# The second half of a w_in product in seven block products, with partial sums kept in PSUM, on one Trainium2 core

## The chip, the core and the metric

One core of a Trainium2 chip runs the whole program; tensors come from and go to HBM. The metric is the device time in microseconds (us) of one execution, of which several were run; the median is compared. 0.2% of it, about 1.5 us, is what counts here as a difference.

## What is computed

A layer norm, attention with a memory over four segments, and a gated MLP that mixes along the sequence. Cut to what matters here (x is 2048 x 1024; `_ln` is a layer norm over the last axis):

```python
h = x + A_ref(_ln(x))                     # 32 heads, 4 segments of 512 tokens, then @ wo
z = gelu(_ln(h) @ w_in)                   # 2048 x 3584
z1, z2 = z[:, :1792], _ln(z[:, 1792:])
g = w_sp @ z2 + b_sp[:, None]             # w_sp is 2048 x 2048
out = h + (z1 * g) @ w_out
```

The part that is changed is the second half of z, `z[:, 1792:]` before its layer norm: a product of 2048 x 1024 by 1024 x 1792, called z2 in the code. The first half is z1.

## The kernel before, in words

The code records every operation of five engines in Python, in the order in which it is called, finds what each has to wait for (by 32-byte cells of SBUF and by whole banks of PSUM, line 87), and then issues each engine's list in that order. So each engine, and each DMA queue, works strictly in the order of the calls. All operations have the line of the recorder, 210, in the profile; they are told apart by the names of their tiles. PE is TensorE, DVE VectorE, ACT ScalarE, POOL GpSimd, SP the engine whose queue issues most DMAs.

The stages, in order:

- **Attention**, n = 0 to 31: segment n // 8 and a group of four heads n % 8. Each round has three sets of logits on PE into banks 0 to 3, three Exp on ACT out of them (`e`), masks on POOL, P times V on PE (`pv`), the division on DVE (`norm`, line 631) into `otok`. Into the gaps of PE go "fills" f1 to f4: projections for the next round, tiles of the wo product of the segment before (`wo`, line 673, which adds x on DVE into `hch`, writes h to `out`, and queues a layer norm) and, in rounds 30 and 31, six groups of z2. `bg_pop` (line 690) moves each queued layer norm one step on: statistics on DVE, then the reciprocal root on POOL (`ln_rstd`, line 491), then the application on DVE (`lno`), followed by a transposing DMA into `HNT`, the normalised h with features on partitions.
- **The end of attention.** After round 31 come `pv(31)` on PE and `norm(31)` on DVE, then four transposing DMAs `oT<-otok`, which the wo product of the last segment reads.
- **z2** (lines 815 and 1019): 64 groups `(k, tc)`, 4 column blocks of 448 by 16 token blocks of 128, each of 8 matmuls of 448 columns, GELU on ACT, statistics on DVE (`z2_stats`). Between the first of them stand the wo tiles of the last segment. Beside it, in `aux`, run the norms of the two weights w_in (first half, on DVE, `sqz`) and w_sp (on ACT, `sj`), the scaling of w_in's first half to 16-bit floats (`wzh`), and differences of blocks of `HNT` (`hn_sum`, line 972).
- **z1** (line 1199): the first half, already by seven block products. With blocks of 512 features and 512 tokens, four output blocks come from seven products of 4 matmuls instead of eight. The factors need sums of blocks: `hn_sum` for h, `sz_sum` (line 985, on POOL) for w_in. DVE adds the products together (`zt<-ps,zt`), reading PSUM. The layer norm of z2 is applied here (`z2_apply`, line 839). w_sp is loaded, scaled and summed.
- **The gate** in two halves (w_sp times z2 by seven products, times z1) and **w_out** in two halves, the second by seven products.

`next_bank` (line 421) hands out the PSUM banks in turn. No operation of POOL touches PSUM here. In z1, bank by bank: product 1 is copied to SBUF by ACT and added to products 6, 7 and 4 by DVE.

Of the kernel before, what the change touches and what calls it, by code (L numbers as in the profile page):

```python
# [14 lines left out]
H = 32  # L15
# [243 lines left out]
def bass_sequential_preLN__memory_aug_infini_attn__mixer_gmlp__prompt_kernel(  # L259
# [31 lines left out]
    class Bump:  # L291
# [4 lines left out]
        def __call__(self, name, shape, dt):  # L296
# [50 lines left out]
    ZSTG = [tens("zstg%d" % i, [128, 448], F32, (134 + 2 * i) * K) for i in range(4)]  # L347
    XCH = [b2("xch%d" % i, [128, D], BF16) for i in range(4)]
# [4 lines left out]
    E = [[b2("e%d%d" % (k, i), [128, 4, w], BF16) for i, w in enumerate((512, 512, 256))] for k in range(2)]  # L353
    TA = b2("ta", [128, 4, 4, 32], F32)
    TM = [b2("tm%d" % i, [128, 4, 4, 32], F32) for i in range(2)]
    V = b2("v", [128, 4, H, 34], BF16)
    OTOK = [b2("otok%d" % i, [128, 4, D], BF16) for i in range(2)]


    WIN = [tens("win%d" % i, [128, 8, 512], BF16, o * K) for i, o in enumerate((46, 54, 190, 198))]  # L360
# [9 lines left out]
          for k, o in ROLES + (("t1", 118), ("t2", 190), ("t3", 22), ("t4", 38))}  # L370
    SS = tens("ss", [128, 4, 8, 128], F16, 30 * K)
    Z1X = tens("z1x", [128, 14, T], F16, 62 * K)
    HT = [{1: Z1X[:, 1:5, 1024:1536], 2: Z1X[:, 1:5, 1536:2048], 3: Z1X[:, 8:12, 1024:1536],
           4: Z1X[:, 8:12, 1536:2048]},
          {1: tens("ht1", [128, 4, L], F16, 190 * K), 2: tens("ht2", [128, 4, L], F16, 194 * K),
           3: tens("ht3", [128, 4, L], F16, 38 * K), 4: tens("ht4", [128, 4, L], F16, 198 * K)}]
    SZ = [tens("sz%d" % i, [128, 4, 128], F16, o * K) for i, o in enumerate((58, 59, 60, 61, 204))]
    ZT = [tens("zt%d" % i, [128, L], F32, o * K) for i, o in enumerate((4, 6, 8, 10, 202, 12))]
# [7 lines left out]
    SQ = b3("sq", [128, 16], F32)  # L386
    SQZ = b3("sqz", [128, 14], F32)
# [18 lines left out]
    SY = [tens("sy%d" % i, [128, 4, 7, 128], F16, o * K) for i, o in enumerate((190, 126))]  # L406
    FIN = [tens("fin%d" % i, [128, 512], BF16, o * K) for i, o in enumerate((37, 11, 12, 13))]
# [399 lines left out]
    CH = [(FH + 448 * k, 448) for k in range(4)]  # L807

    def win_load(k):
        lo, w = CH[k]  # L810
        sp.dma_start(WIN[k][:, :, 0:w], wcols(B_w_in, lo, lo + w))

    zs, zq, staged = [], [], []

    def z2_group(k, tc, stage=None):
        s, tcl = divmod(tc, 4)
        b = next_bank()
        wi = WIN[k]
        mm8(PS[:, b, 0:448], lambda i: HNT[s][:, i, tcl * 128:(tcl + 1) * 128], lambda i: wi[:, i, 0:448])
# [6 lines left out]
    def z2_gelu(k, tc, src):  # L826
        act.activation(Z2[:, tc, k * 448:(k + 1) * 448], src, ACTF.Gelu_apprx_tanh)
        zs.append((k, tc))

    def z2_stats():  # L830
        k, tc = zs.pop(0)
        dve.bn_stats(ZST[:, tc, k, :], Z2[:, tc, k * 448:(k + 1) * 448])
        if k == 3:
# [13 lines left out]

    LAST = NSEG * NQ - 1
    for n in range(LAST + 1):
# [15 lines left out]
        elif c < 6:  # L865
            f3, f4 = [("wo", s - 1, c - 2, 0)], [("wo", s - 1, c - 2, 1)]
        elif c == 6:
            f3, f4 = [("z2", 0, 4, 0)], [("z2", 0, 5, 1)]
        else:
            f1, f2 = [("z2", 0, 6, 2)], [("z2", 0, 7, 3)]  # L870
            f3, f4 = [("z2", 0, 0)], [("z2", 0, 1)]
# [14 lines left out]
        if n == 0:  # L886
# [3 lines left out]
            f3 = [("vmm", 0, 0, 1, 6, 2, 8), ("vout", 0, 0, 1, 6)]  # L890
        logits(n, 0)
# [24 lines left out]
        bg_pop()  # L916
        if n == 0:
# [616 lines left out]
```

## Time and profile before

| | us |
|---|---|
| median of 3 runs (754.47 to 755.01) | 754.56 |
| profiled execution, own time | 753.9 |
| its span, first to last instruction | 752.2 |
| busy in the span: PE / DVE / ACT / POOL | 747.5 / 559.3 / 421.3 / 297.0 |
| attention, up to the end of `pv(31)` | 0 to 302.8 |
| z2 and the last wo tiles | 302.8 to 404.3 |
| z1 | 404.3 to 490 |

The profile is a page and a trace of one execution. A timeline's line gives the start in us, the duration, the engine, the operation, the output and inputs by tile name, their shapes and the count of instructions merged into the line; in square brackets is the idle time of the engine before it, and who ended it. A matmul's duration is longer than the distance to the next matmul, since they are pipelined. The chain of waits follows the end of the program back to its beginning, at each step to whatever was waited for.

### The profile page before, as it was taken

The page shows a single profiled execution, that of the slowest core. Times are in us where ns is not written, and L with a number is a line of the kernel's source. Part 1 is how long each engine was busy: PE and PEld are TensorE (multiplying, and loading weights), DVE is VectorE, ACT ScalarE, POOL GpSimd, SP SyncE. Part 2 cuts the span into 40 slices and gives each one's busy share as a digit, 9 for nine tenths or more (in the row PEclk, how much of TensorE's full clock was granted, in tenths as well). Part 3 has the DMA queues.
Part 4 walks back from the last instruction along what each step waited for, and adds up shares of the span by engine and source line. Part 5 has one row for each costly group of instructions (what it writes and reads, how often), then busy time and mean ns, then how long its engine had stood idle before and what let it go on. Part 6 is the DMA issues. An engine that isn't in the chain of part 4 may idle for free.

```text
span 752.2 us, 13510 instructions
## 1 busy us (share of the span) xinstructions
PE 747.5 (99%) x5470; PEld 358.8 (48%) x5470; DVE 559.3 (74%) x1013; ACT 421.3 (56%) x519; POOL 297.0 (39%) x450
## 2 busy tenths in 40 slices
PE   8999999999999999999999999999999999999998
PEld 4445455555555445545554444444444444444444
DVE  5585589768975576667988796997885465989776
ACT  6777877787777767324994879733231445300000
POOL 2564456555654334010049888622220001222342
PEclk9999999999999999999999999999999999999999
DMA  9654556444523331669650027320019950001211
GB/s 303 177 159 88 85 82 135 99 74 91 120 58 81 118 84 44 162 178 262 196 169 0 1 45 138 56 98 1 0 23 155 269 185 28 0 1 43 78 50 57
DMA packets 136783, 75.09 MB, mean 100 GB/s; under 512 B 98064, under 2 KB 126480, under 8 KB 136720
## 3 DMA queue, kind: packets, MB, share of 16 engines
q1 hardware_dynamic: 129184, 67.14, 36.9%
q10 hardware_dynamic: 7536, 7.08, 3.3%
q8 instruction: 43, 0.70, 0.4%
q14 instruction: 20, 0.16, 0.1%
HBM read 42.74 MB, written 8.39 MB: 68 GB/s over the span
## 4 chain that ended last, share of the span: by engine, by line
PE 98%; DMA 1%; ACT 0%; DVE 0%; ACTq 0%; DVEq 0%; issue 0%
PE ps L210 98%; DMA wv<-in_A_wv_dram 1%; ACT L210 0%; DVE fin L210 0%; ACTq L210 0%; DVEq L220 0%; ACT rdm L210 0%
## 5 line engine op out<-in xcount | busy, mean ns | idle before, releaser
L210 ACT ACTIVATE e<-ps 128x2048 bf16<-128x2048 f32 (+1 forms) x96 | 152.6, 1590 | 41.7 <-PE ps L210 41.5
L210 POOL TENSOR_SCALAR_AFFINE_SELECT e<-e 128x512 bf16<-128x512 bf16 x128 | 90.6, 720 | 131.6 <-ACT e L210 131.5
L210 PE MATMUL ps<-win,hnT 128*128 128x448 bf16 x512 | 98.4, 352 | 0.0
L210 POOL TENSOR_TENSOR tmp_s1b<-tmp_s,brow 128x512 f32<-128x512 f32 x28 | 36.9, 1322 | 121.3 <-DVE tmp_u L210 62.5
L210 PEld LDWEIGHTS ps<-win,hnT 128*128 128x128 bf16 x512 | 49.6, 98 | 46.3 <-issue 0.2
L210 PE MATMUL ps<-xnT,wk 128*128 128x512 bf16 x256 | 60.8, 380 | 0.0
L210 PE MATMUL ps<-xnT,wq 128*128 128x512 bf16 x256 | 60.5, 379 | 0.0
L210 PE MATMUL ps<-wv,xnT 128*128 128x512 bf16 x256 | 59.7, 380 | 0.3 <-DVE xnT L210 0.3
L210 DVE TENSOR_TENSOR zt<-ps,zt 128x512 f32<-128x512 f32 x70 | 48.2, 690 | 15.6 <-PE ps L210 12.3
L210 PE MATMUL ps<-wo,oT 128*128 128x512 bf16 x256 | 58.0, 379 | 0.0
L210 ACT ACTIVATE z<-ps 128x448 bf16<-128x448 f32 x60 | 30.4, 545 | 33.4 <-PE ps L210 33.4
L210 PE MATMUL ps<-w_out,z1T 128*128 128x512 bf16 x224 | 48.6, 379 | 0.0
L210 PEld LDWEIGHTS ps<-v,e 128*128 128x128 bf16 x1280 | 38.8, 96 | 14.0 <-issue 6.5
L210 DVE BATCH_NORM_STATS2 zst<-z 128x6 f32<-128x448 bf16 x64 | 37.7, 607 | 7.8 <-ACT z L210 7.8
L210 DVE RECIPROCAL rd<-ps 128x16 f32<-128x16 f32 x32 | 8.0, 250 | 47.1 <-PE ps L210 46.9
L210 PE MATMUL ps<-v,e 128*128 128x33 bf16 x1280 | 42.2, 178 | 0.0
L210 ACT ACTIVATE tmp_s<-ps,invy 128x512 f32<-128x512 f32 x7 | 4.8, 688 | 64.9 <-POOL tmp_s1b L210 36.1
L210 POOL TENSOR_TENSOR sz<-wzh 128x512 f16<-128x512 f16 x28 | 34.4, 1230 | 16.9 <-DVE wzh L210 8.5
L210 PEld LDWEIGHTS ps<-wo,oT 128*128 128x128 bf16 x256 | 24.0, 98 | 27.6
L210 PEld LDWEIGHTS ps<-xnT,wk 128*128 128x128 bf16 x256 | 22.6, 98 | 29.9 <-issue 5.0
L210 ACT ACTIVATE z1T<-zt,inv 128x512 bf16<-128x512 f32 x42 | 29.0, 716 | 13.1 <-DVE zt L210 13.1
L210 PEld LDWEIGHTS ps<-wv,xnT 128*128 128x128 bf16 x256 | 23.1, 98 | 27.2 <-DVE xnT L210 0.7
(204 smaller groups left out, 1462.3 us busy)
## 6 DMA issues: line engine op xcount, KB each, us to landing
sj<-in_B_w_sp_dram SPq DMA_DIRECT2D x16, 512.0 KB, 3.5
xch<-in_A_x_dram SPq DMA_DIRECT2D x16, 256.0 KB, 3.5
xr<-in_A_x_dram SPq DMA_DIRECT2D x16, 256.0 KB, 4.0
out_dram<-hch SPq DMA_DIRECT2D x16, 256.0 KB, 2.5
win<-in_B_w_in_dram SPq DMA_DIRECT2D x4, 896.0 KB, 5.4
wz<-in_B_w_in_dram SPq DMA_DIRECT2D x6, 512.0 KB, 8.3
wo<-in_A_wo_dram SPq DMA_DIRECT2D x1, 2048.0 KB, 8.5
fin<-out_dram ACTq DMA_DIRECT2D x16, 128.0 KB, 3.0
```

The source lines that it names most:

```text
L210: ins = getattr(e, op.name)(*op.args, **op.kw)
```

## The change

z2 is made by the same seven-product scheme as z1, on blocks of 512 features, 512 tokens (in tiles of 128) and 448 columns. Eight of the 64 plain groups stay (six of them in attention), the other 56 output blocks come from 14 groups of seven products. `z2_step(q, k)` issues product k of group q; a list sorted by 7 q + OFF2[k] interleaves neighbouring groups, and `at(n, ...)` hangs other work behind its n-th step. Of the sums between products, some are made by PE itself: ACT copies product 1 from its bank into a second bank, and product 6 is accumulated onto it, then 7 or 4; ACT keeps copies after 6 and 5, and DVE adds them in after 7 and 3. Where a bank had not been written over the full width, one dummy matmul is issued into it first. Banks are handed out from a list `free`, and given back after products 2, 3 and 4.

For this w_in's second half, too, is scaled to 16-bit floats (`w_half`), and its blocks are summed (`w_sum`, `w_perm`). The scale must be known in attention, so w_in and seven sixteenths of w_sp are loaded there in pieces once more, or earlier, and their norms (a maximum on DVE, or squares on ACT) are taken there; the rest of w_sp follows in z2 by half rows. `hn_sum` for the first half of the tokens moves into attention, that for the second into z2. In z1 the feature blocks are taken in another order (`FC`), two of w_in's four scalings and some 17 statistics of z2 are done there. Many buffers lie at other addresses. Unchanged functions that only moved in the file are left out here.

```diff
...
-    ZSTG = [tens("zstg%d" % i, [128, 448], F32, (134 + 2 * i) * K) for i in range(4)]
-    XCH = [b2("xch%d" % i, [128, D], BF16) for i in range(4)]
+    ZSTG = [tens("zstg%d" % i, [128, 448], F32, int(o * K)) for i, o in enumerate((201, 202.75, 204.5, 144))]
...
-    HT = [{1: Z1X[:, 1:5, 1024:1536], 2: Z1X[:, 1:5, 1536:2048], 3: Z1X[:, 8:12, 1024:1536],
-           4: Z1X[:, 8:12, 1536:2048]},
-          {1: tens("ht1", [128, 4, L], F16, 190 * K), 2: tens("ht2", [128, 4, L], F16, 194 * K),
-           3: tens("ht3", [128, 4, L], F16, 38 * K), 4: tens("ht4", [128, 4, L], F16, 198 * K)}]
+    HT = [{1: Z1X[:, 0:4, 1024:1536], 2: Z1X[:, 0:4, 1536:2048], 3: Z1X[:, 4:8, 1024:1536],
+           4: Z1X[:, 4:8, 1536:2048]},
+          {1: tens("ht1", [128, 4, L], F16, 4 * K), 2: tens("ht2", [128, 4, L], F16, 8 * K),
+           3: tens("ht3", [128, 4, L], F16, 38 * K), 4: tens("ht4", [128, 4, L], F16, 200 * K)}]
+    WIN = {0: tens("win0", [128, 8, 448], BF16, 46 * K), 2: tens("win2", [128, 8, 448], BF16, 54 * K),
+           1: Z1T[:, 0:8, 0:448], 3: Z1T[:, 0:8, 448:896]}
+    WIH = {0: tens("wih0", [128, 8, 448], F16, 46 * K), 2: tens("wih2", [128, 8, 448], F16, 54 * K),
+           1: Z1X[:, 0:8, 0:448], 3: Z1X[:, 0:8, 448:896]}
+
+    WSO = {"a": 190, "b": 193.5, "c": 197, "d": 126, "e": 178, "f": 174.5, "g": 101, "h": 94, "i": 97.5}
+    WSO = {k: tens("ws" + k, [128, 4, 448], F16, int(o * K)) for k, o in WSO.items()}
+    WS = {pc: {k: WSO[x] for k, x in zip((2, 3, 4), ks)} for pc, ks in
+          (((0, 0), "abc"), ((1, 0), "abd"), ((0, 1), "efg"), ((1, 1), "hig"))}
+    ZP = [[tens("zp%d%d" % (p, i), [128, 448], F32, (o + 2 * i) * K) for i in range(6)]
+          for p, o in enumerate((162, 105))]
...
+    NB = [tens("nb%d" % i, [128, T], BF16, int(o * K)) for i, o in
+          enumerate((22, 26, 181.5, 185.5, 197.5, 201.5, 189.5, 193.5, 14))]
...
+    free = []
+
+    def next_bank(hold=False):
+        if free:
+            b = free.pop(0)
+            if not hold:
+                free.append(b)
+            return b
...
-        wi = WIN[k]
-        mm8(PS[:, b, 0:448], lambda i: HNT[s][:, i, tcl * 128:(tcl + 1) * 128], lambda i: wi[:, i, 0:448])
+        mm8(PS[:, b, 0:448], lambda i: HNT[s][:, i, tcl * 128:(tcl + 1) * 128], lambda i: WIH[k][:, i, :])
...
-        act.activation(Z2[:, tc, k * 448:(k + 1) * 448], src, ACTF.Gelu_apprx_tanh)
+        act.activation(Z2[:, tc, k * 448:(k + 1) * 448], src, ACTF.Gelu_apprx_tanh, scale=INV[1][:])
-        if k == 3:
+        nz[tc] = nz.get(tc, 0) + 1
+        if nz[tc] == 4:
...
+    def scale_in(src, n, w):
+        m = src[:, 0:n]
+        dve.scalar_tensor_tensor(m, m, float(w), m, ALU.mult, ALU.mult)
+        pool.tensor_copy(SQB[:, 0:src.shape[1]], src[:])
...
+    FC = (2, 3, 0, 1, 4, 5, 6, 0, 1, 2, 3, 4, 5, 6)
...
+    def w_half(c, eng=dve):
+        if eng is act:
+            act.activation(WIH[c][:], WIN[c][:], ACTF.Copy, scale=SC[1][:])
+            return
+        eng.tensor_single_scalar(WIH[c][:], WIN[c][:], SC[1][:], ALU.mult)
+
+    def w_blk(i, j, c):
+        return WIH[c + 2 * i][:, 4 * j:4 * j + 4, :]
+
+    def w_sum(c, k, ws=None, eng=dve):
+        if k == 1:
+            eng.tensor_tensor(w_blk(1, 0, c), w_blk(1, 0, c), w_blk(1, 1, c), ALU.add)
+            return
+        a, b = {3: (w_blk(0, 0, c), w_blk(1, 0, c)), 2: (w_blk(1, 1, c), ws[3][:]), 4: (w_blk(0, 1, c), ws[2][:])}[k]
+        eng.tensor_tensor(ws[k][:], a, b, ALU.subtract)
+
+    def w_perm():
+        ws = WS[1, 1]
+        pool.tensor_tensor(ws[2][:], w_blk(1, 0, 1), w_blk(0, 0, 1), ALU.subtract)
+        pool.tensor_tensor(ws[3][:], w_blk(1, 1, 1), ws[2][:], ALU.subtract)
...
+    def piece_load(buf, o, i):
+        if o is SQ:
+            sp.dma_start(buf[:], B_w_sp[i * 128:(i + 1) * 128, :])
+        else:
+            r, h = divmod(i, 2)
+            sp.dma_start(buf[:, 0:FH], B_w_in[r * 128:(r + 1) * 128, h * FH:(h + 1) * FH])
+
+    def piece_norm(buf, o, i, q):
+        v = buf[:] if o is SQ else buf[:, 0:FH]
+        if q is act:
+            i += 9 * (o is SQ)
+            act.activation(v, v, ACTF.Square, accum_out=o[:, i:i + 1])
+        else:
+            dve.tensor_reduce(out=o[:, i:i + 1], in_=v, axis=mybir.AxisListType.X, op=ALU.max,
+                              apply_absolute_value=True)
+
+    pieces = {}
+    for i, (n, k, q) in enumerate(((8, 0, dve), (8, 1, dve), (9, 8, dve), (14, 0, dve), (15, 1, dve), (16, 0, dve),
+                                   (17, 1, dve), (22, 2, dve)) + tuple((x, x % 2, act) for x in range(10, 14))
+                                  + tuple((x, 2 + x % 2, act) for x in range(18, 22))):
+        pieces.setdefault(n, []).append((NB[k], SQZ, i, q))
+    for i, (n, k, q) in enumerate(((23, 4, dve), (24, 3, dve), (24, 5, dve), (25, 4, dve), (26, 5, act), (27, 6, act),
+                                   (28, 7, act))):
+        pieces.setdefault(n, []).append((NB[k], SQ, i, q))
...
-            f3, f4 = [("z2", 0, 4, 0)], [("z2", 0, 5, 1)]
+            f3, f4 = [("z2", 2, 0, 0)], [("z2", 2, 4, 1)]
         else:
-            f1, f2 = [("z2", 0, 6, 2)], [("z2", 0, 7, 3)]
-            f3, f4 = [("z2", 0, 0)], [("z2", 0, 1)]
+            f1, f2 = [("z2", 2, 1, 2)], [("z2", 2, 5, 3)]
+            f3, f4 = [("z2", 0, 0)], [("z2", 0, 4)]
...
+        piece_norms(n, act)
...
+        piece_norms(n, dve)
...
-            win_load((n - 24) // 2)
+            win_load(n - 24)
+        if n == 24:
+            pool.memset(ONES[:], 1.0)
+            pool.memset(MHZ[:], -0.5)
+            scale_in(SQZ, 8, 1.0)
+        if n == 25:
+            scale_of(16)
+        if n == 26:
+            scale_end(1)
+            w_half(0)
+        if n == 28:
+            w_half(2)
+        if n == 29:
+            w_sum(0, 3, WS[0, 0])
+            w_sum(0, 2, WS[0, 0])
+        if n == 30:
+            w_sum(0, 4, WS[0, 0])
+            hn_sum(0, 1, 0)
+            hn_sum(0, 1, 1)
+            xr_load(4 * (NSEG - 1))
+            win_load(1)
+            win_load(3)
+        if n == LAST:
+            hn_sum(0, 2, 0)
+            hn_sum(0, 2, 1)
+            hn_sum(0, 3, 0, pool)
+            hn_sum(0, 3, 1, pool)
+            w_sum(0, 1)
+            hn_sum(0, 4, 0)
+            hn_sum(0, 4, 1)
     pv(LAST)
...
+    free.extend((0, 1, 2, 6, 3, 4, 7, 5))
+    G2 = [(0, 0, 2), (0, 0, 3)] + [(p, c, t) for p, c in ((0, 1), (1, 0), (1, 1)) for t in range(4)]
+    OFF2 = {1: -6, 6: 0, 5: 1, 2: 2, 7: 4, 4: 10, 3: 12}
+    zb2, wide, late, jobs2 = {}, set(range(6, 8)), [], {}
+
+    def z2_step(q, k):
+        p, c, t = G2[q]
+        u2, u3 = ZP[p][q % 3][:], ZP[p][3 + q % 3][:]
+        ka = {1: w_blk(0, 0, c), 2: w_blk(0, 1, c), 4: w_blk(1, 1, c), 5: w_blk(1, 0, c)}
+        ka = ka[k] if k in ka else WS[p, c][{3: 4, 6: 2, 7: 3}[k]][:]
+        kb = {1: hb(0, 0, p), 2: hb(1, 0, p), 3: hb(1, 1, p), 4: HT[p][4], 5: HT[p][1], 6: HT[p][2], 7: HT[p][3]}[k]
+        r = {1: 0, 2: 0, 6: 1, 7: 1, 4: 1, 5: 2, 3: 2}[k]
+        if k in (1, 5):
+            zb2[q, r] = next_bank(True)
+        if k == 1:
+            zb2[q, 1] = next_bank(True)
+        v = [PS[:, zb2[q, x], 0:448] if (q, x) in zb2 else None for x in range(3)]
+        for i in range(4):
+            pe.matmul(v[r], kb[:, i, t * 128:(t + 1) * 128], ka[:, i, :], start=(k in (1, 5) and i == 0),
+                      stop=(i == 3), skip_group_check=True)
+        wide.add(zb2[q, r])
+        if k in (2, 3, 4):
+            free.append(zb2[q, r])
+        todo, late[:] = late[:], []
+        if k == 1:
+            if zb2[q, 1] not in wide:
+                pe.matmul(v[1], kb[:, 0, 0:128], ka[:, 0, :], start=False, stop=False, skip_group_check=True)
+                wide.add(zb2[q, 1])
+            act.activation(v[1], v[0], ACTF.Copy)
+        elif k == 6:
+            act.activation(u2, v[1], ACTF.Copy)
+        elif k == 5:
+            act.activation(u3, v[2], ACTF.Copy)
+        elif k == 7:
+            dve.tensor_tensor(u3, v[1], u3, ALU.add)
+            late.append(lambda: z2_gelu(c + 2, 8 * p + 4 + t, u3))
+        elif k == 2:
+            z2_gelu(c, 8 * p + t, v[0])
+        elif k == 4:
+            z2_gelu(c + 2, 8 * p + t, v[1])
         else:
+            dve.tensor_tensor(u2, v[2], u2, ALU.add)
+            late.append(lambda: z2_gelu(c, 8 * p + 4 + t, u2))
+        for f in todo:
+            f()
+
+    def at(x, f, *a):
+        jobs2.setdefault(x, []).append((f, a))
+
+    def wo_tile(tcl):
+        for half in range(2):
+            wo(NSEG - 1, tcl, half)
+            wide.add(free[-1])
+            bg_pop()
+
+    def sj_load(i):
+        r, h = 7 + i // 2, i % 2
+        sp.dma_start(SJ[i % 3][:], B_w_sp[r * 128:(r + 1) * 128, 1024 * h:1024 * (h + 1)])
+
+    def sj_norm(i):
+        if i % 2:
+            dve.tensor_reduce(out=SQ[:, 4 + i // 2:5 + i // 2], in_=SJ[i % 3][:], axis=mybir.AxisListType.X, op=ALU.max,
+                              apply_absolute_value=True)
+        else:
+            act.activation(SJ[i % 3][:], SJ[i % 3][:], ACTF.Square, accum_out=SQ[:, 16 + i // 2:17 + i // 2])
+
+    def plain(tc):
+        z2_group(0, tc)
+        wide.add(free[-1])
+
+    at(0, plain, 1)
+    at(0, plain, 5)
+    at(0, w_half, 3, pool)
+    at(2, w_half, 1)
+    at(7, w_sum, 1, 3, WS[0, 1])
+    at(8, w_sum, 1, 2, WS[0, 1])
+    at(9, w_sum, 1, 1, None, pool)
+    for i in range(4):
+        at(8 + 2 * i, wo_tile, i)
+    for i in range(18):
+        at(18 + 3 * i, sj_load, i)
+        at(26 + 3 * i, sj_norm, i)
+    for i in range(5):
+        at(16 + i, bg_pop)
+    at(17, w_sum, 1, 4, WS[0, 1])
+    at(16, w_perm)
+    at(17, w_sum, 0, 4, WS[1, 0], pool)
     for k in range(8):
+        at(22 + 2 * k, hn_sum, 1, (1, 2, 3, 4)[k // 2], k % 2, pool if k in (4, 5) else dve)
+    at(26, wz_load, 1)
+    for h in range(2):
+        at(52 + 4 * h, wz_half, 1, h, pool)
+        at(92 + 2 * h, wz_half, 0, h)
     for k in (1, 2, 3, 4):
+        at(76 + 2 * k, sz_sum, 0, k)
+    for k in (0, 2, 3):
+        at(75, wz_load, k)
+
+    at(91, scale_in, SQ, 13, T)
+
+    seq2 = sorted((7 * q + OFF2[k], q, k) for q in range(len(G2)) for k in OFF2)
+    credit = 0.0
+    for n, (x, q, k) in enumerate(seq2):
+        z2_step(q, k)
+        for f, a in jobs2.pop(n, ()):
             f(*a)
+        credit = min(credit + (0.3 if n < 40 else 0.62), 2)
+        if credit >= 1 and len(zs) > 1:
             z2_stats()
+            credit -= 1
+    for f in late:
+        f()
...
-    for g in range(8):
+    for g in range(11):
         on(g, 6, lambda: zq and z2_apply())
-        on(g, 4, lambda: zq and z2_apply(True))
-    for k in range(4, 8):
-        on(*((4, 6), (5, 6), (6, 6), (7, 6))[k - 4], hn_sum, 1, (1, 2, 3, 4)[k // 2], k % 2)
-    on(1, 7, scale_of, 0, 16, None)
+        if g < 8:
+            on(g, 4, lambda: zq and z2_apply(True))
+    for k in range(4):
+        on(k // 2, (2, 3)[k % 2], wz_half, (2, 3)[k // 2], k % 2)
+    for g in range(11):
+        for k in (4, 3):
+            on(g, k, lambda: zs and z2_stats())
+    on(1, 7, scale_of, 25)
...
```

## The prediction

> **What bounds the kernel.** I read the chain of waits first, then a sum by stretches, then the timeline at the two places that the change moves.
>
> ```profile
> PE 98%; DMA 1%; ACT 0%; DVE 0%; ACTq 0%; DVEq 0%; issue 0%
> ```
> ```profile
> 8.79 740.31 PE ps L210 x5431
> ```
> ```profile
> 302.80:404.30 101.50, 101.50 (x535) 51.65 (x532) 82.84 (x144) 59.33 (x92) 19.21 (x39) 1.00 0.63 179
> 404.30:490.00 85.70, 85.70 (x399) 38.51 (x397) 69.89 (x102) 68.43 (x90) 70.12 (x69) 1.00 0.30 53
> ```
> The chain is one unbroken run of TensorE from 8.79 us on. The columns of the stretches are PE, PEld, DVE, ACT, POOL: from 302.8 (end of attention) to 404.3 (first z1 matmul) POOL has worked 19 of 101.5 us. So a matmul taken away counts in full, and any wait put in front of TensorE counts in full too.
>
> ```profile
> 302.78 6.21 PE L210 MATMUL ps<-win,hnT 128*128 128x448 bf16 x32
> ```
> ```profile
> 442.79 1.44 POOL L210 TENSOR_TENSOR sz<-wzh 128x512 f16<-128x512 f16 x1 [0.56 <-PE ps L210]
> 443.14 1.65 DVE L210 TENSOR_TENSOR ht<-hnT,ht 128x1024 f16<-128x1024 bf16 x1
> ...
> 444.31 1.49 POOL L210 TENSOR_TENSOR sz<-sz,wzh 128x512 f16<-128x512 f16 x1
> ...
> 445.77 1.16 POOL L210 TENSOR_TENSOR sz<-wzh 128x512 f16<-128x512 f16 x1
> ```
> ```profile
> 385.35 0.68 DVE L210 TENSOR_TENSOR ht<-hnT,hnT 128x1024 f16<-128x1024 bf16 x1
> ```
> 32 matmuls take 6.21 us, the last of them 0.352: (6.21 - 0.352)/31 = 0.189 us each. The same `hn_sum` on DVE takes 0.68 us alone and 1.65 us beside a POOL operation: it ends at 444.79, 0.55 after POOL's at 444.24, and POOL's next one, 1.49 in place of 1.16 us, waits for it in turn. The two take turns by whole instructions. In the timeline this holds for POOL operations of 0.64 to 2.0 us, and for DVE operations that read two SBUF tensors or convert or normalise 16-bit data (`lno`, `wzh`); sums with a PSUM operand (`zt<-ps,zt`) pass.
>
> **What goes.** After attention the kernel issues 58 plain groups of 8 matmuls, 464. The new one issues 2 plain groups, 14 groups of 7 x 4, and one dummy (bank 1 is not yet `wide`): 409. 55 x 0.189 = **-10.4 us**. The four wo tiles (64 x 0.216) stay. The sum over SQZ moves from this stage into attention, 0.03 us.
>
> **ACT in the new stage.** Per group (28 x 0.189 = 5.3 us) there are 3 copies and 4 GELUs; two GELUs in a row start 0.42 to 0.47 apart (303.15: two in 0.96), so 3.1 us, and 1.2 squares of 1024 (sj row: 2048 take 1.80 + 0.09) 1.2 us: 4.3 of 5.3. The seed of product 6 comes 4 slots (3.0 us) after product 1. ACT's order, DVE's adds included, is behind by less; cost 0. **DVE** has about 75 us in the 91 us that remain, so on average it keeps up; what matters is who holds it.
>
> **POOL's long instructions.** `sz` sums of 512 start 1.11 us apart (410.47, 411.58). The new POOL sums of 1024 take 2.2, those of 1792 3.9 us. `w_half(3, pool)` converts 3584 elements, a POOL form that isn't here. Its nearest one-input row is the mask (512 in 0.58 to 0.64): 4.05 us; by the only scaled row (`maskg`, 256 in 0.965) 13.5 us; below 3.7 (the `maskg` copy, 1024 in 1.05) I see no row. I take 4.0, since the mask is 16-bit and contiguous like it.
>
> **Place A, the end of attention.**
> ```profile
> 298.44 2.22 POOL L210 TENSOR_SCALAR_AFFINE_SELECT e<-e 128x512 bf16<-128x512 bf16 x3 [1.81 <-ACT e L210]
> ...
> 300.49 0.69 DVE L210 TENSOR_TENSOR tm<-ps,rdm 128x512 f32<-128x512 f32 x1
> ...
> 304.19 0.69 DVE L210 TENSOR_TENSOR otok<-ta,tm 128x512 bf16<-128x512 f32 x1
> ...
> 304.91 5.36 SPq L210 DMA_TRANSPOSE oT<-otok  x4
> ```
> POOL is free at 300.66, DVE at 301.18. POOL gets `hn_sum(0,3)` twice, then `w_half(3)`; DVE gets `hn_sum(0,2)` twice, the sum of W blocks (1792: 2.2 us of the 4096 row `th<-bh,bh` gives 1.0), `hn_sum(0,4)` twice, and only then `norm(31)`. In turns: POOL 300.7 to 302.85, DVE 303.4, POOL 305.6, DVE 306.15, POOL 310.2, DVE's W sum 311.1, the last two 312.3, norm (1.9 us: 302.97 to 304.88) 314.2, first oT transpose landed 3.3 us later (its row among the DMA issues) 317.5. TensorE: 302.78, nine steps of 0.757, dummy 0.19, two plain groups 3.03: at the first wo tile by 312.8. It waits **4.7 us** in all (3.6 of it already at product 5, which reads that W sum). Without turns DVE would be done by 306.5, the transposes by 309.8, and the wait is 0. The W loads, issued some 296 on an SP that is idle after 295.5, land in about 8 us; if later, POOL's turn and DVE's swap, and the chain ends at the same 317.5.
>
> **Place B, after the last wo tile (t = 0 at its last matmul).** DVE: add 0.6, `lno` 0.5, statistics 1.4, aggregate 0.1: 2.7; POOL's rstd 0.85: 3.6. Next on POOL is `w_perm`, two sums of 3.9; next on DVE are `ln_apply` and `w_sum(1,4)`, both of the kind that takes turns. POOL, which needs no signal, is first: 7.5; apply 7.8; POOL 11.7; W sum 12.6; then the add of product 7(2) 13.2. TensorE needs that add before 4(2), which writes its bank, nine steps on: 6.8. It waits **6.4 us**. Queued behind on ACT are the GELU of that add, and behind it the copies that 7(3) and 6(4) need. If apply is first, one turn of 3.9 us falls away: 2.6 us.
>
> **Slow restart.** The first eight matmuls of the kernel (`ps<-etmp`) last 628 ns, others of 512 columns 379. They start 0.427 apart against 0.216: 1.7 us if TensorE comes back so after a wait. Nothing here shows such a wait; 0 to 1.7 at each place. I take 1.7 once, for the longer. The Trainium skill ("TensorE: Matmul & The Clock Gate", Part 1) states that a window of about 3.4 us without work halves the clock, until another of work; by it B pays surely and A perhaps, 1.7 or 3.4 by these rows. The granted clock in this profile is 1.00 in every stretch, so no row here agrees or disagrees.
>
> **z1.** 17 z2 statistics (0.53) and four `wz_half` come in, four `hn_sum` (1.65 each, and TensorE never waited for them) go out. DVE per group of 6.05 us: five adds 3.05, apply 0.65, two statistics 1.07, aggregate 0.18: 4.9. Groups 1 and 2 get 0.74 to 1.39 us twice over: 7.0. The add that product 7 needs would then be late by 1.6 and 0.8 us. Between 0 and 2.4 I take **1.2**. POOL (4.5 of sums, 0.85, 0.5 of 6.05) stays just under.
>
> **Attention.** ACT's 1792-element squares (w_out row: 1.60 + 0.09) stand in its 1.76 us hole before each first exp (192.12), the 2048-element ones (1.9) in 2.18 (285.20). DVE's reductions (1.12 per 1024: 1.9 to 2.2) find its 1.5 to 3 us idle per head group, mostly before `rd` (46.9 us in 22 waits). 7.2 MB more of loads meet 109 GB/s where 303 is reached, and 0.6 us each on an SP that waits most of the time. Cost 0, at most 3 us (23 pieces of 0.13, the overshoot of 1.69 + 0.2 over 1.76). The moved buffers carry no instruction; where one would wait for an old reader, the reader is a stage back.
>
> **Sum.** -10.4 + 4.7 + 6.4 + 1.7 + 1.2 = +3.6. The profiled execution took 753.9 (span 752.2 and 1.7 around it): 757.5. The runs' median, 754.56, is 0.7 above it: **758.2**, own range 754.5 to 763.
>
> A rule of the Trainium skill speaks against this change: "SBUF — State Buffer", Who interferes with whom, says that DVE with two SBUF inputs, or in a two-port mode, and a POOL instruction that reads SBUF lock each other out for a whole instruction, the one that starts first going on. The rows agree up to 2.0 us; if no operation were held up for longer than that, A would cost 2.4 and B 2.6 with no slow restart, and the result would be 750.4; by the rule it is the forecast.
>
> **Rivals.** (1) The other side: POOL's turns don't reach TensorE, because they end early or DVE's operations pass. For it: TensorE never waited for a turn in this profile. Against it: no DVE queue here had more than one long turn ahead of an add. -10.4 + 1.0 = 744.5, or 745.2 against the median; the sign changes where the waits come to less than 10.4. Chance 0.22. (2) `ln_apply` gets in before `w_perm`: B is 2.6, taken as too short for a slow restart: -10.4 + 4.7 + 2.6 + 1.2 = -1.9, 752.7 (749 to 755). Chance 0.20. (3) POOL converts at the `maskg` rate: 9.5 us more at A: 767.7. Chance 0.13. Forecast 0.45.
>
> **Chances and range.** 0.2% is 1.5 us, about what a measurement of this kernel can tell from no change. Faster: rival 1 and 0.12 of rival 2, 0.34. Same: 0.08 of rival 2, 0.03 of the forecast, 0.11. Slower: 0.55. The range leaves out rival 3 and the lower end of rival 1: 744.5 to 763.
>
> **What would show it.** TensorE idle before its fifth new product and before the first wo tile, released by DVE and by the oT transpose; idle some 7 us after the last wo tile, released by a DVE add on PSUM; DVE operations of 4 us ending half a microsecond after a POOL one; a granted clock under 1.00 there. If the stage from the end of attention to z1 lasts 91 us in place of 101.5, the turns cost nothing and I am wrong at A and B; if attention is longer, wrong in its holes.

## The result, and the profile after

The changed kernel takes **774.86 us** (median of 4 runs, 774.54 to 775.67) against 754.78 of the kernel before (4 runs, 754.47 to 755.36): a ratio of 1.0267, 95% interval 1.0249 to 1.0284. The prediction was 758.2, with a range to 763.0. Slower was right; the size was 17 us short. The profiled execution took 774.59 us, span 772.9.

First the chain of waits of the kernel after. Before, it was TensorE for 98%.

```profile
PE 84%; DVE 12%; issue 2%; DMA 1%; ACT 1%; POOL 0%; DVEq 0%
```

Then the stretches from the end of attention to z1, and z1 (columns as before: PE, PEld, DVE, ACT, POOL, then the granted clock).

```profile
303.31:418.67 115.36, 97.32 (x480) 47.08 (x477) 102.46 (x136) 63.43 (x120) 58.95 (x40) 0.93 0.40 110
418.67:509.94 91.27, 86.54 (x395) 36.98 (x393) 83.14 (x128) 64.72 (x88) 72.31 (x74) 1.00 0.29 50
```

They lasted 101.63 and 84.87 us before; attention ends 0.55 us later, and the gate (84.61 before, 84.62 after) and w_out (175.39 in both, to the start of its last matmul) last as long as before. So +0.55 + 13.74 + 6.39 = +20.7 us, all of the difference, is up to the end of z1. TensorE's waits, in us: in total, times, longest (the one at the very start, the same in both kernels, left out).

```profile
PE ps L210 <- DVE ta L210: 9.0, 1, 9.0
PE ps L210 <- DVE zp L210: 7.3, 2, 5.7
PE ps L210 <- DVE zt L210: 4.7, 8, 1.7
...
PE ps L210 <- ACT zp L210: 0.9, 2, 0.7
PE ps L210 <- DVE hch L210: 0.8, 1, 0.8
```

**Place A.** Timeline of the kernel after:

```profile
305.88 10.68 POOL L210 TENSOR_SCALAR z1x<-z1T,sc 128x3584 f16<-128x3584 bf16 x1
306.31 1.08 DVE L210 TENSOR_TENSOR wih<-wih 128x1792 f16<-128x1792 f16 x1
307.31 9.52 DVE L210 TENSOR_TENSOR z1x<-hnT,z1x 128x1024 f16<-128x1024 bf16 x2
...
317.24 0.69 DVE L210 TENSOR_TENSOR ta<-ps,rd 128x512 f32<-128x512 f32 x1
317.99 3.17 PE L210 MATMUL ps<-wih,hnT 128*128 128x448 f16 x8 [9.01 <-DVE ta L210]
```

`w_half(3, pool)` takes 10.68 us. DVE's two `hn_sum(0,4)`, 1.3 us alone, last 9.52 and end with it; `norm(31)` follows, and TensorE starts 0.06 us after `ta`, at product 1 of group 1. The banks that the division reads are among the last three that the new stage takes up.

**Place B.**

```profile
348.59 3.57 POOL L210 TENSOR_TENSOR wsh<-z1x 128x1792 f16<-128x1792 f16 x1
348.66 3.79 DVE L210 TENSOR_SCALAR lno<-hch,mv,rs 128x1024 bf16<-128x1024 bf16 x1 [0.49 <-POOL rs L210]
...
352.24 3.62 POOL L210 TENSOR_TENSOR wsi<-z1x,wsh 128x1792 f16<-128x1792 f16 x1
352.36 4.45 DVE L210 TENSOR_TENSOR wsg<-z1x,wse 128x1792 f16<-128x1792 f16 x1
...
356.73 1.14 DVE L210 TENSOR_TENSOR zp<-ps,zp 128x448 f32<-128x448 f32 x2
357.40 1.68 PE L210 MATMUL ps<-z1x 128*128 128x448 f16 x4 [5.67 <-DVE zp L210]
```

`lno` (0.5 us alone) ends 0.3 behind POOL's first sum, the W sum (1.1 alone) 0.95 behind its second; the add of 7(2) and TensorE's 4(2) come after, as forecast.

**The clock.** Stretches of 3.41 us around place A; the first pair after the comma is TensorE's busy time, and the third figure from the end the granted clock.

```profile
310.27:313.68 3.41, 0.00 (x0) 0.00 (x0) 3.41 (x1) 0.00 (x0) 3.41 (x1) 1.00 0.00 0
313.68:317.10 3.42, 0.00 (x0) 0.00 (x0) 3.39 (x4) 0.00 (x0) 2.88 (x1) 0.50 0.00 0
317.10:320.51 3.41, 2.52 (x7) 1.04 (x8) 3.09 (x5) 0.53 (x1) 0.00 (x0) 0.50 0.19 39
320.51:323.92 3.41, 3.41 (x10) 1.37 (x9) 1.23 (x3) 0.63 (x1) 0.00 (x0) 0.50 1.01 189
323.92:327.34 3.42, 3.42 (x17) 1.47 (x15) 2.01 (x2) 2.04 (x4) 2.42 (x1) 1.00 0.68 156
```

TensorE works 2.52 + 3.41 us at half clock here, 0.66 + 3.41 after place B: half of each is lost, 3.0 and 2.0 us.

**z1.**

```profile
431.12 0.68 DVE L210 TENSOR_TENSOR zt<-ps,zt 128x512 f32<-128x512 f32 x1
431.72 1.55 DVE L210 TENSOR_SCALAR wzh<-wz,sc 128x2048 f16<-128x2048 bf16 x1
...
433.19 0.61 DVE L210 BATCH_NORM_STATS2 zst<-z 128x6 f32<-128x448 bf16 x1
433.73 0.67 DVE L210 TENSOR_TENSOR zt<-ps,zt 128x512 f32<-128x512 f32 x1
434.32 0.61 DVE L210 BATCH_NORM_STATS2 zst<-z 128x6 f32<-128x448 bf16 x1
434.85 0.67 DVE L210 TENSOR_TENSOR zt<-ps,zt 128x512 f32<-128x512 f32 x1
435.58 1.04 PE L210 MATMUL ps<-z1x,sz 128*128 128x512 f16 x4 [1.73 <-DVE zt L210]
```

The scaling and the statistics stand between DVE's adds, and TensorE waits for the second add. Counting what each wait loses (the distance of two matmul starts less the usual one), z2 is -10.4 + 9.2 (A) + 0.95 (`hch`, the first wo tile) + 5.83 (B) + 0.85 and 1.83 (two waits after B) + 5.0 (half clock) = +13.3 of the 13.74; z1 has five losses of over 0.4 us: 1.90, 0.79, 0.61, 1.01 and 0.62, 4.9 of 6.39.

### The profile page after: what moved, and what is told of

Same layout as the page of the kernel before. It is cut to its first block, busy times and chain, and to the rows that moved or that the text cites. A ratio compares the mean times of both kernels' runs of the same rounds, so it can differ in the third digit from the quotient of the medians.

```text
span 772.9 us, 13557 instructions
## 1 busy us (share of the span) xinstructions
PE 745.5 (96%) x5415; PEld 353.5 (46%) x5415; DVE 626.2 (81%) x1056; ACT 441.2 (57%) x566; POOL 342.0 (44%) x459
## 4 chain that ended last, share of the span: by engine, by line
PE 84%; DVE 12%; issue 2%; DMA 1%; ACT 1%; POOL 0%; DVEq 0%
PE ps L210 84%; DVE zt L210 3%; DVE z1x L210 2%; DVE zst L210 1%; DVE ht L210 1%; DVE wsg L210 1%; DVE sqz L210 1%; DVE t1h L210 0%; DMA hnT<-lno 0%; DVE zp L210 0%; DMA xch<-in_A_x_dram 0%; DVE wzh L210 0%; DVE tm L210 0%; DVE z2h L210 0%; ACT e L210 0%
## 5 line engine op out<-in xcount | busy, mean ns | idle before, releaser
L210 ACT ACTIVATE z1T<-zt,inv 128x512 bf16<-128x512 f32 x42 | 29.2, 716 | 24.1 <-DVE zt L210 24.1
L210 POOL TENSOR_TENSOR sz<-wzh 128x512 f16<-128x512 f16 x28 | 33.9, 1211 | 10.6 <-PE ps L210 10.6
L210 ACT ACTIVATE qk<-ps 128x512 bf16<-128x512 f32 x48 | 28.7, 599 | 12.7 <-PE ps L210 12.7
L210 PE MATMUL ps<-qk 32*128 32x128 bf16 (+3 forms) x512 | 34.5, 302 | 0.1
L210 PEld LDWEIGHTS ps<-xnT,wq 128*128 128x128 bf16 x256 | 23.4, 97 | 22.9 <-issue 0.2
L210 ACT ACTIVATE z<-zp,inv 128x448 bf16<-128x448 f32 x28 | 18.7, 668 | 26.5 <-DVE zp L210 26.2
```

Source lines behind the costliest of these rows:

```text
L210: ins = getattr(e, op.name)(*op.args, **op.kw)
```

## The experiments

Each kernel is compared with runs of the kernel before on the same chip. "Stage" is the time from the start of the last `pv(31)` matmul to the first z1 matmul.

**1. The conversion on DVE.**

```diff
-    at(0, w_half, 3, pool)
+    at(0, w_half, 3)
```

> One edit to the changed kernel: the fourth piece of w_in (w_half(3), 3584 elements per partition) is scaled on DVE instead of POOL. Theory (the long POOL conversion is what holds DVE at the end of attention, and through DVE's sums the norm that gives TensorE its bank): the conversion takes about 1.2 us on DVE as its twin at 318.58 did, the sum hn_sum(0,4) that lasted 9.5 us lasts at most 2.5, the wait of 9.0 us ended by ta falls under 3 us, and the 10.2 us at half clock behind it goes; the stage from the end of attention to z1 gets 11 to 14 us shorter (115.4 to about 102 to 104), the whole 774.9 to about 761 to 764. Rival (DVE's five sums ahead of the norm are too many whoever holds them, or the half clock comes anyway): the wait stays above 5 us and the time above 767.

Measured: 764.25 us, stage 104.25, no half clock there. TensorE's wait for `ta` is 0.8 us, and the two sums take their own time:

```profile
308.85 1.28 DVE L210 TENSOR_TENSOR z1x<-hnT,z1x 128x1024 f16<-128x1024 bf16 x2
```

The stage is 11.1 us shorter, for 8.3 of the wait (9.2 less 0.94) and 3.0 of the half clock. The theory holds: this one line carried 11.1 us of the stage's losses, which come to 24.1 (the 13.7 by which the stage had grown, and the 10.4 that went). The whole gained 10.6, the profiled execution 9.6, since the load of `wv` kept TensorE waiting 1.5 us at its start.

**2. The division first.** POOL keeps its conversion.

```diff
-            w_sum(0, 1)
-            hn_sum(0, 4, 0)
-            hn_sum(0, 4, 1)
     pv(LAST)
+    w_sum(0, 1)
+    hn_sum(0, 4, 0)
+    hn_sum(0, 4, 1)
```

> One edit to the changed kernel: the last attention division norm(31) comes ahead of the W sum and of hn_sum(0,4) on DVE; POOL still converts w_half(3) in 10.7 us. Theory (what TensorE waited for was the bank that the division reads): ta is done by about 306, the wait ended by ta goes, and the next late thing is the W sum that product 5 reads or hn_sum(0,4) that product 4 reads, which now run beside POOL's conversion and end with it, about 317 to 319; TensorE then waits there for 2 to 7 us, released by DVE wih or z1x in place of ta; the time is 764 to 773. Rival (the turn at POOL is no matter once the division is out of it): no wait above 1 us there, time about 761 to 763.

Measured: 775.23 us, nothing gained, and above the theory's range too. The wait is 9.1 us long still, now for the W sum; and the division itself was held up:

```profile
306.67 9.38 POOL L210 TENSOR_SCALAR z1x<-z1T,sc 128x3584 f16<-128x3584 bf16 x1 [0.41 <-DMA z1T<-in_B_w_in_dram]
306.72 0.24 DVE L210 RECIPROCAL rd<-ps 128x16 f32<-128x16 f32 x1
307.00 8.20 DVE L210 TENSOR_TENSOR rd<-rd,omg 128x16 f32<-128x16 f32 x1
315.24 0.69 DVE L210 TENSOR_TENSOR ta<-ps,rd 128x512 f32<-128x512 f32 x1
...
317.71 1.68 PE L210 MATMUL ps<-wih,z1x 128*128 128x448 f16 x4 [9.08 <-DVE wih L210]
```

The reciprocal reads PSUM and passes. The product `rd<-rd,omg`, 16 elements, 0.17 us alone, reads two SBUF tensors and lasts 8.20 us. The theory had `ta` done by 306, and the rival rested on it too; both fell on this one instruction: not the size of the DVE operation counts but whether it is of the kind that takes turns. The Trainium skill ("SBUF — State Buffer", Who interferes with whom) says so of a DVE instruction with two SBUF inputs; the row shows it for the smallest operation of the stage.

**3. POOL's W sums later.**

```diff
-    at(16, w_perm)
-    at(17, w_sum, 0, 4, WS[1, 0], pool)
+    at(40, w_perm)
+    at(46, w_sum, 0, 4, WS[1, 0], pool)
```

> One edit to the changed kernel: POOL's w_perm (two sums of 1792) moves from behind step 16 to behind step 40, its w_sum(0,4) from 17 to 46, past the last wo tile's layer norm and DVE's W sum. Theory (place B is POOL's long sums holding lno and the W sum ahead of the add of product 7(2)): lno takes 0.6 us in place of 3.8, the W sum about 1.1 in place of 4.4, the wait of 5.8 us ended by zp goes, and the 6.8 us at half clock behind it too: 5.8 + 3.4, about 9 us off, some 765 to 767 (place A stays as it is); up to 2 us may come back where the sums now stand beside hn_sum(1,t). Rival (the last wo tile's layer norm and the DVE queue are late by themselves): a wait of over 3 us stays there, time 769 or more.

Measured: 768.05 us, stage 108.5: 6.9 off. Place B is gone, and the new one is smaller:

```profile
348.56 0.55 DVE L210 TENSOR_SCALAR lno<-hch,mv,rs 128x1024 bf16<-128x1024 bf16 x1 [0.49 <-POOL rs L210]
349.02 1.09 DVE L210 TENSOR_TENSOR wsg<-z1x,wse 128x1792 f16<-128x1792 f16 x1
350.03 1.15 DVE L210 TENSOR_TENSOR zp<-ps,zp 128x448 f32<-128x448 f32 x2
...
357.82 4.03 POOL L210 TENSOR_TENSOR wsh<-z1x 128x1792 f16<-128x1792 f16 x1
...
358.86 3.53 DVE L210 TENSOR_TENSOR ht<-hnT,ht 128x1024 f16<-128x1024 bf16 x1
```

5.83 + 2.0 less the waits that come in its place (0.88, 1.68 and 1.17, for 0.85 and 1.83 before): the theory holds. The expectation was 1 to 3 us lower: it took half of the 6.8 us at half clock, but TensorE worked only 4.07 us of them and lost 2.0, and the new waits are 1.05 longer than those they replace.

**4. What makes POOL's conversion slow.**

```diff
-    at(0, w_half, 3, pool)
+    at(0, lambda: pool.tensor_copy(WIH[3][:], WIN[3][:]))
...
+    def wz_half_i(q, h, eng):
+        eng.tensor_single_scalar(WZH[q][:, 4 * h:4 * h + 4], WZ[q][:, 4 * h:4 * h + 4], 8.0, ALU.mult)
...
-        at(52 + 4 * h, wz_half, 1, h, pool)
+        at(52 + 4 * h, (wz_half_i, wz_half)[h], 1, h, pool)
```

> A measurement of POOL's rate, with three forms in the changed kernel's own places: w_half(3) is a plain copy bf16 to 16-bit float (so the scale is left out of a quarter of the second half of w_in), wz_half(1,0) is multiplied by a constant in the instruction instead of the scale from SBUF (its scale is left out), and wz_half(1,1) stays as it was; the output is not the reference's. In the changed kernel 3584 elements took 10.68 us (2.98 ns each) and 2048 took 5.90 (2.88 ns). If it is the scale read from SBUF that is slow, the copy takes 3.5 to 4.1 us and the constant form 2.0 to 2.4; if it is the change of type, the copy takes 10 to 11 us; if it is the multiplication form, the copy is short and the constant form stays near 5.9.

```profile
307.17 3.35 POOL L210 CAST z1x<-z1T 128x3584 f16<-128x3584 bf16 x1 [0.23 <-DMA z1T<-in_B_w_in_dram]
...
358.78 5.72 POOL L210 TENSOR_SCALAR wzh<-wz 128x2048 f16<-128x2048 bf16 x1
379.79 5.45 POOL L210 TENSOR_SCALAR wzh<-wz,sc 128x2048 f16<-128x2048 bf16 x1
```

It is the multiplication form: the copy with the same change of type takes 0.93 ns an element, the multiplication 2.7 to 2.9, by a constant (5.72 us) or by a scale from SBUF (5.90 at the same step in the kernel after) alike.

This kernel leaves the scale out at two places, so only its times are read; the stage is 107.15 us, 8.2 shorter, with no half clock at place A. What the short conversion leaves there is the prediction's own chain: the W sum waits behind POOL, TensorE waits for it at product 5, and then for `ta`.

```profile
307.42 4.05 DVE L210 TENSOR_TENSOR wih<-wih 128x1792 f16<-128x1792 f16 x1
...
311.52 0.93 PE L210 MATMUL ps<-wih,z1x 128*128 128x448 f16 x4 [2.21 <-DVE wih L210]
...
313.83 1.69 PE L210 MATMUL ps<-wih,hnT 128*128 128x448 f16 x8 [1.37 <-DVE ta L210]
```

The two lose 2.37 and 1.53 us and the wait for `hch` 0.94: 4.84, where the prediction had 4.7 with a conversion of 4.0 us.

**5. The statistics of z1.**

```diff
-        credit = min(credit + (0.3 if n < 40 else 0.62), 2)
+        credit = min(credit + (0.3 if n < 40 else 0.62 if n < 60 else 1.0), 2)
```

> One edit to the changed kernel: from step 60 of z2 on, one statistics instruction per step is allowed in place of 0.62, so that most of the 17 that ran in z1 run in z2. Theory A (z1's small waits at 470 to 510 come from the statistics and the applications that follow them late): the waits of 0.61, 1.01 and 0.62 us in z1's second half go, the first two (1.90 and 0.79) stay, z1 is 2 to 3 us shorter (91.3 to 88.5 or 89); z2 is 0 to 5 us longer, since DVE there is busy 6.9 of 7 us from 366 to 408. Theory B (they come from the w_sp sums t1h and t2h beside POOL alone): z1 keeps them, 91.

Measured: z1 87.44 (3.8 shorter), stage 120.74 (5.4 longer), 777.13 us in all. The losses of 0.61 and 1.01 went, and three of 0.36 with them, so the statistics made them; the first two fell to 0.55 and 0.70, more than expected, and the last, 0.62, stayed, against theory A. In z2 they cost more, a loss of 3.05 us with half clock behind it among it: DVE has no room there either.

**6. The scalings of z1.**

```diff
+        if eng is act:
+            act.activation(WZH[q][:, 4 * h:4 * h + 4], WZ[q][:, 4 * h:4 * h + 4], ACTF.Copy, scale=SC[1][:])
+            return
...
-        on(k // 2, (2, 3)[k % 2], wz_half, (2, 3)[k // 2], k % 2)
+        on(k // 2, (2, 3)[k % 2], wz_half, (2, 3)[k // 2], k % 2, act)
```

> One edit to the changed kernel: the four scalings of w_in's first half that stand in z1's first two groups (wz_half(2) and (3), 0.84 to 1.55 us each on DVE) go to ACT. Theory (z1's first waits, 1.90 and 0.79 us ended by zt, are DVE's adds queued behind these scalings): both go, z1 is about 2.7 us shorter, 88.6; the later ones stay. Rival (ACT, busy 4.4 of 6 us per group there, now brings its copies of product 1 late, which the adds read): the waits stay at 2 us or more, ended by zt behind a late ACT copy, z1 is 90 to 92.

Measured: z1 88.39, as expected; the losses of 1.90 and 0.79 are gone, the later ones stay. The whole: 772.77.

**7. z2 without long POOL work.** Experiment 1, `w_perm` with the engine as its argument, and

```diff
-    at(9, w_sum, 1, 1, None, pool)
+    at(9, w_sum, 1, 1)
...
-    at(16, w_perm)
-    at(17, w_sum, 0, 4, WS[1, 0], pool)
+    at(40, w_perm, dve)
+    at(46, w_sum, 0, 4, WS[1, 0])
...
-        at(22 + 2 * k, hn_sum, 1, (1, 2, 3, 4)[k // 2], k % 2, pool if k in (4, 5) else dve)
+        at(22 + 2 * k, hn_sum, 1, (1, 2, 3, 4)[k // 2], k % 2)
...
-        at(52 + 4 * h, wz_half, 1, h, pool)
+        at(52 + 4 * h, wz_half, 1, h)
```

> The changed kernel with all long POOL work between the end of attention and step 76 moved to DVE: w_half(3), w_sum(1,1), w_perm (behind step 40), w_sum(0,4) of the second row (behind step 46), hn_sum(1,3) and wz_half(1); only hn_sum(0,3) stays on POOL. Theory (the turns cost more than the work itself: DVE's operations of 16-bit data took some 27 us longer than alone): DVE takes on about 9 us of work and loses the turns; no wait above 1.5 us between 303 and the start of z1, no half clock, the stage 92 to 95 us in place of 115.4, the whole 751 to 755. Rival (DVE, with 77 us of work of its own and 9 more in 91, becomes the bound): a chain of waits on zp in the second half, stage 97 or more.

```profile
303.49:399.39 95.90, 92.24 (x480) 45.71 (x477) 87.60 (x145) 63.57 (x120) 17.43 (x30) 1.00 0.49 132
```

DVE does 8.4 us more of work (1.15 + 1.04 + 2.18 + 1.08 + 1.4 + 1.5, by its rows) and is busy 14.9 us less than in the kernel after (102.46); no half clock. 756.04 us (8 runs), 1.0024 of before (1.0013 to 1.0035): the theory's mechanism, at 1 us more than it had for the whole and the stage, and with one wait above its 1.5. Its losses are 0.93 (`ta`), 0.95 (`hch`), and 1.60 and 0.67 ended by ACT's copy of product 1.

**8. The single edits together.** Experiments 1, 3 and 6, and

```diff
-        at(52 + 4 * h, wz_half, 1, h, pool)
+        at(52 + 4 * h, wz_half, 1, h)
```

> The changed kernel with four edits: w_half(3) on DVE, w_perm and w_sum(0,4) on POOL but behind steps 40 and 46, wz_half(1) on DVE, wz_half(2) and (3) on ACT in z1. If the costs found apart add up: 764.3 (w_half alone) less 6.9 (w_perm late) less 1 to 2 (no 5.9 us conversion beside hn_sum) less 2.7 (z1) = 752.5 to 754, as fast as the kernel before. If they do not add up (DVE's queue late anyway): 756 or more.

Measured: 756.66 (8 runs), 1.0029 of before (1.0018 to 1.0040). They don't add up, and the expectation's other branch came out: the stage is 99.56, with 0.91, 1.68 and 1.16 beside POOL's later W sums, as in experiment 3, and then 1.03 and 0.68 for ACT's copy, which the kernel after doesn't have. Against 7 (stage 95.90, with `w_sum(1,1)` and `hn_sum(1,3)` on DVE too) a later place on POOL is worth less than a place on DVE.

**9. A version that beats both.** Experiments 6 and 7, and

```diff
             hn_sum(0, 3, 1, pool)
             w_sum(0, 1)
-            hn_sum(0, 4, 0)
-            hn_sum(0, 4, 1)
     pv(LAST)
+    hn_sum(0, 4, 0)
+    hn_sum(0, 4, 1)
...
-    at(7, w_sum, 1, 3, WS[0, 1])
-    at(8, w_sum, 1, 2, WS[0, 1])
-    at(9, w_sum, 1, 1)
+    at(9, w_sum, 1, 3, WS[0, 1])
+    at(9, w_sum, 1, 2, WS[0, 1])
+    at(10, w_sum, 1, 1)
```

> All long POOL work of z2 on DVE as in z2_no_pool, the four scalings of z1's first groups on ACT, and two changes of order: hn_sum(0,4) behind norm(31), and the W sums for the second columns (w_sum(1,3), (1,2), (1,1)) two or one steps later, behind the first wo tile. If costs add up: 756.0 (z2_no_pool) less 2.9 (the z1 edit alone) less 0.95 (wait ended by ta) less 0.95 (wait ended by hch) = 751.2 (750.5 to 752.5), 0.4% faster than the kernel before. If the two small waits only move on to the next product or tile: 752.5 to 753.5.

Measured: **752.26 us** (11 runs) against 754.57 (21 runs), ratio 0.9972 (0.9963 to 0.9981): 0.3% faster than the kernel before. It is inside its range of 750.5 to 752.5. The wait for `ta` is gone, that for `hch` isn't. TensorE's waits, those at the very start left out:

```profile
PE ps L210 <- DVE zt L210: 2.3, 6, 0.8
PE ps L210 <- ACT ps L210: 1.9, 2, 1.4
...
PE ps L210 <- DVE hch L210: 0.8, 1, 0.8
```

**10. The waits for ACT's copy: the w_sp norms earlier.** On top of 9:

```diff
-        at(18 + 3 * i, sj_load, i)
-        at(26 + 3 * i, sj_norm, i)
+        at(14 + 5 * i // 2, sj_load, i)
+        at(21 + 5 * i // 2, sj_norm, i)
```

> As mend2, and the 18 norms of half rows of w_sp (9 squares on ACT, 9 maxima on DVE) are spread over steps 21 to 63 of z2 in place of 26 to 77. Theory (the waits of 1.60 and 0.67 us at 369.8 and 376.7 that ACT's copy of product 1 ended are squares of 1.24 us standing ahead of it on an ACT that has 4.5 us of its own in each 5.3): one or both go, 1 to 2 us off mend2, 749.5 to 750.5. Rival (DVE's adds, which the GELU ahead on ACT waits for, are what is late): no gain, or waits of the same size at other places, 751 to 753.

**11. The squares in step with the groups.** On top of 9:

```diff
-        at(18 + 3 * i, sj_load, i)
-        at(26 + 3 * i, sj_norm, i)
+        x = 74 if i == 16 else 22 + 7 * (i // 2) + 3 * (i % 2)
+        at(x - 8, sj_load, i)
+        at(x, sj_norm, i)
```

> As mend2, and the squares of half rows of w_sp on ACT come every seventh step, each right behind ACT's copies of a product 1 (steps 22, 29, ... 71, 74), the maxima on DVE three steps later each. Theory (the waits of 1.60 and 0.68 us ended by ACT's copy of product 1 come where a square of 1.24 us happens to be queued ahead of that copy, since squares come every sixth step and groups every seventh): both go, 2 us off mend2: 750 to 750.5, 0.55% below the kernel before. Rival (ACT waits for DVE's adds there, and the square is only what happens to stand in its wait): no gain, 752 or above, waits of over 1 us ended by ACT ps or ACT zp stay.

**12. The first wo tile's halves one step apart.** On top of 11, where `wo_half` issues one half:

```diff
-    for i in range(4):
+    at(8, wo_half, 0, 0)
+    at(9, wo_half, 0, 1)
+    for i in range(1, 4):
         at(8 + 2 * i, wo_tile, i)
```

> As mend4, and the two halves of the first wo tile of the last segment are issued one step apart. Theory (the wait of 0.95 us ended by hch there is the second half taking the only free bank, which the first half's sum on DVE has just to release): the wait goes, 0.95 us off mend4. Rival (the sum is late since DVE's W conversions stand ahead of it): the wait moves to the second half or the next product, same time.

Measured for 10, 11 and 12: 755.16 us (1.0008 of before, 0.9998 to 1.0017), 755.65 (1.0020, 1.0010 to 1.0030) and 754.16 (0.9999, 0.9990 to 1.0008), 11 runs each. Both new orders of the squares are worse than 9: five losses of 0.56 to 1.60 us, and three of 0.51 to 2.74, ended by ACT, the longest with 3.4 us of half clock behind it. But that longest one has a cause that neither theory nor rival had. From the trace of 11:

```profile
380.21 1.22 DVE L210 TENSOR_REDUCE sq<-sj 128x1 f32<-128x1024 bf16 x1 [3.23 <-DMA sj<-in_B_w_sp_dram]
...
384.11 1.57 PE L210 MATMUL ps<-wsh,ht 128*128 128x448 f16 x4 [2.58 <-ACT ps L210]
```

A maximum on DVE waits 3.23 us for the load of its half row; DVE's add behind it (381.88), then ACT's GELU and copies (382.52 to 384.06), then TensorE are late. Experiment 12 has the same wait (3.51), 10 has two such that come to 2.0 us (one on ACT, one on DVE), and 9 has none. So these kernels don't measure the order of the squares alone. With that loss and its half clock (2.74 and 1.7 us) put aside, the stage of 11 would be 94.55 us by my estimate, against 94.99 in 9: not the 2 us of the theory. A loss of 1.29 us that stays in 11 (364.81) has no square ahead of it; there ACT's GELU waits 2.09 us for DVE's add, as the rival has it. For the two waits of 9 it was not settled which operation of the ring is first late (ACT's copy waits for the GELU ahead of it, that for DVE's add, that for statistics ahead of it). In the last one the wait for `hch` is gone, as its theory said: the second half of the tile had taken the bank of the first.

## Why the prediction was wrong in size

- **What goes, -10.4: right.** With TensorE's losses put aside (0.93 + 0.95 + 1.60 + 0.67 = 4.15), the stage of experiment 7 comes to 91.75, forecast 91.2.
- **Place A, 4.7: measured 9.2, and 0.95 for `hch`.** The step that failed is "I take 4.0, since the mask is 16-bit and contiguous like it". `w_half(3, pool)` took 10.68 us in the kernel after, where a W sum ran at its start, and 9.38 in experiment 2, where none did (2.6 ns an element): nearer to the upper bound of 13.5 that rival 3 had. Had it been a copy, 4.0 would have stood (3.35), and the place would have cost 4.84 where the sum had 4.7 (experiment 4). So the mechanism was right and this term was mis-sized. One turn of the chain behind it fell otherwise in the kernel after: the W sum passed in its own time (306.31, 1.08) though the conversion's record begins before it; by the prediction's order, with 9.4 in it, `ta` would have come some 1 us later than it did (my estimate, by its own terms). Why this turn differs between the two kernels was not tested. And what TensorE missed first was the bank of the division, not the oT transposes.
- **Place B, 6.4: measured 5.83,** released as forecast. Not forecast were 0.85 and 1.83 us behind it, the second after POOL's `wz_half(1)` (5.90 us) has held up a sum of the second half (`ht`, 3.69 us for 0.67). I followed only the first two places of POOL's long operations.
- **Slow restart, 1.7 once: measured 3.0 + 2.0.** It was paid at both places. The estimate took eight matmuls; the trace has 17 at place A (7 + 10) and 12 at B. The rule cited there, that a window without work is followed by half clock until another of work, agrees in its length of 3.41 us, but not in what it takes: see the last section.
- **z1, 1.2: measured 6.4.** The sum by groups saw groups 1 and 2 only, and took 1.2 between 0 and 2.4. Experiment 6 puts 2.9 us on the four scalings, experiment 5 shows 2.7 us (0.61, 1.01 and three of 0.36) as the statistics' in later groups, which the sum had at 4.9 of 6.05 us and so at no cost: ahead of the loss of 1.01 an application, put off by the statistics, stands right before the sums of w_sp. The last 0.62 stayed in both experiments and was not explained.
- **ACT, 4.3 of 5.3 us, cost 0: too low.** GELUs with the scale start 0.51 us (out of PSUM) or 0.56 to 0.58 (out of SBUF) ahead of the next operation, where the sum had 0.42 to 0.47 for all four. In the kernel after, other waits hid it; once they are gone, 1.6 + 0.67 us are ended by ACT (7 and 9).
- **Attention, 0: measured +0.55.** 0.43 of it is one wait for ACT's copy `v` (at 248.87), which the kernels of the experiments looked at have too. They end attention up to 1.5 us later still, since the load of `wv` at the start came late in some executions; that is not the change's.

Together: 5.5 (A) + 2.1 (B) + 3.3 (clock) + 5.2 (z1) + 0.55 (attention) + 0.4 (rest of z2) = 17.1, the distance from +3.6 to +20.7. Rival 1, that the turns don't reach TensorE, was wrong. So was rival 2: POOL came first. Rival 3 was right in its mechanism, and I had given it 0.13, as if the bounds of 3.7 and 13.5 stood equally far; no row showed the form, and the only row of a POOL multiplication spoke for the upper end.

## What to carry to other kernels

Price a POOL instruction not by its own time but by what it holds up: the first DVE operation with two SBUF inputs, conversion or normalisation that is queued beside it can wait until POOL is nearly or quite done, however small it is, and all that stands behind it on DVE waits with it. Here moving 8.4 us of work onto an already busy DVE took 14.9 us off DVE's busy time and 18.8 off the whole. Before work is handed to an engine, look for a row of the same form: on POOL a copy and a multiplication of one tensor took 3.35 and 9.38 us. And when a stage is tightened, the engines that were merely busy (here DVE and ACT) take over the waits; count the load in each group of steps, with durations of the same form.

## What the runs showed of the hardware

- POOL's rates for 16-bit data: copy with change of type 0.93 ns an element (3584 in 3.35 us), sum of two tensors 2.0 (1792 in 3.57), multiplication by one scalar 2.6 to 2.7 (3584 in 9.38, 2048 in 5.45). The rows of 10.68 and 5.90 us for the same work stand where a DVE operation of the kind that takes turns was running at their start.
- Turns of up to 8.2 us for a DVE operation of 16 elements. Maxima (1.20 us), statistics (0.57 to 0.62) and sums with a PSUM operand (0.56 to 0.62) were not held up beside POOL's multiplication of 5.46 us (from 386.91 on in the kernel after).
- The half clock needs no empty window. In the traces here, windows of 3.41 us at full clock in which TensorE had 1.54 us of work or less were followed by one at half clock, and such with 1.61 or more by one at full clock. The first from experiment 2 (two rows), then experiment 4 (two rows):

```profile
370.35:373.76 3.41, 1.54 (x9) 0.42 (x6) 3.41 (x7) 1.16 (x3) 1.22 (x1) 1.00 0.28 91
373.76:377.17 3.41, 3.41 (x10) 1.38 (x11) 3.41 (x6) 3.41 (x8) 0.00 (x0) 0.50 0.37 118
```
```profile
311.09:314.51 3.42, 1.61 (x8) 0.72 (x9) 3.32 (x8) 0.54 (x1) 0.00 (x0) 1.00 0.00 0
314.51:317.92 3.41, 3.41 (x20) 1.76 (x18) 3.20 (x5) 2.02 (x4) 0.00 (x0) 1.00 0.66 127
```

The Trainium skill ("TensorE: Matmul & The Clock Gate", Part 1) speaks of an idle window of about 3.4 us; by these rows a loss of about 2 us inside one window can be enough, and one of the same size that falls across two is not (1.83 us at 371.0 of the kernel after, no half clock). Where the limit lies between 1.54 and 1.61 us of work was not tested by itself.
